# Chunk 1's q and k transposed by DMA instead of TensorE, with a new order of the work

## The chip, the cores and the metric

The kernel runs on one core of a Trainium2 chip. The metric is the device time of one execution in microseconds (us). A core has TensorE (matmuls and transposes; PE in the profile, PEld its weight loads), VectorE (DVE), ScalarE (ACT), GpSimd (POOL), SyncE (SP) and 16 DMA engines. SyncE, ScalarE and GpSimd each issue DMAs on a queue of their own (SPq, ACTq, POOLq).

## The reference, cut to what matters

A retention recurrence over 768 steps for 4 batches and 8 heads of 64, followed by a two-layer feed-forward with a tanh gelu over the 3072 tokens.

```python
for t in range(S):
    state = gamma[None, :, None, None] * state + np.einsum('bhd,bhe->bhde', k[:, :, t], v[:, :, t])
    y[:, :, t] = scale * np.einsum('bhd,bhde->bhe', q[:, :, t], state)
...
x = attn_out.transpose(0, 2, 1, 3).reshape(B * S, H * D)      # [3072, 512]
h = x @ w_in                                                   # [3072, 2048]
g = 0.5 * h * (1.0 + np.tanh(c * (h + 0.044715 * h * h * h)))
out = g @ w_out                                                # [3072, 512]
```

## The kernel before

**Tiling.** Time is cut into 6 chunks (c) of 128 steps; each chunk has 4 batches (b). w_in is cut into 4 column blocks and w_out into 4 row blocks (j). Inside a chunk, the recurrence is done as matrix work: a masked product of queries and keys, its product with the values, and the part that comes from the state. The 512 tokens of a chunk then go through the feed-forward. From chunk 0 (j = 2, 3) and chunk 1 on, both layers use a seven-product scheme for 2x2 blocks (sums of blocks ahead of the products); chunk 0 uses plain products for j = 0, 1 and for the second layer.

**The order.** The program is a string of words, ORDER (lines 16 to 138), read in the loop at lines 682 to 700. Each word calls one helper, which issues one or a few instructions. Nothing is reordered later: the place of a word in the string is the place of its instructions on their engine or queue, and an engine waits at an instruction until its inputs and its output buffer are there. A word's last letter V, A, P or S names DVE, ScalarE, GpSimd or SyncE; "@n" gives the buffer; "<word" adds a dependency on another word, used to keep GpSimd and DVE apart. The words of this study:

- L:q,c,b,e (line 330) loads 256 KB of q, k or v on queue e into one of 13 buffers "r". LC and LI load constants, LWI:j (262, two DMAs of 256 KB) and LWO:j (270, one of 512 KB) load a block of w_in or w_out on GpSimd's queue, where the fp32 weights become fp16. HOLD (296) is a two-element DMA.
- PREP (342) scales or converts a loaded tile to fp16; q and k of one (c,b) share a tile qk. EA multiplies by the decay mask (382, DVE).
- T:c,b (357) transposes q and k of one batch on TensorE, eight transposes of 128x128 into PSUM (a "bank"); ET (364) copies the result into the tile qkT. DT:c,b (367) does both with one DMA transpose on SyncE's queue, from qk to qkT. Before, chunks 0 and 1 use T and ET, chunks 2 to 5 use DT.
- A:c,b (374) is keys times queries from qkT, eight matmuls of half the rows. YP (390), YI (406) and SS (435) are the part from the state, the part inside the chunk and the state's update; EP, EY and ES copy their results.
- HB:j,b (486) is 16 matmuls of 128 columns, plain first layer for chunk 0. M1:c,j,n (539) is the n-th of seven products of the first layer, four matmuls of 256 columns; CP (567) and D1 (571) combine them, G and GB (575, 500) apply the gelu on ScalarE. O0:b,j (594) is the plain second layer of chunk 0, four matmuls of 512 columns; M2 (614) the second layer of the other chunks.
- WI, WO (320, 324) are sums of weight blocks, four per j and layer; SX and SG sums of blocks of x and g.
- ZERO and SPIN give TensorE 11 matmuls on zeros at the start.

All matmuls run through line 223, transposes on TensorE through 362, two-operand element work through 220, copies through 215 (ScalarE) and 217, gelu through 466, loads through 332, w_in through 266, w_out through 271, DMA transposes through 369.

**The order around the change.** First loads: SyncE takes k(0,1), constants, k(0,0), q(0,0), v(0,1), v(0,2); ScalarE q(0,1), k(0,2), q(0,2), q(0,3), k(0,3). GpSimd's queue takes, in order: LWI:2, v(0,0), v(0,3), LWI:0, LWI:3, LWI:1, then eight q and k of chunk 1, LWO:0, LWO:1, four v of chunk 1, LWO:2, k(2,3), q(2,3), LWO:3, seven loads of chunk 2. SyncE's own next words are three loads or holds and then DT of chunk 2.

Of the kernel before, what the change touches and what calls it, by code (L numbers as in the profile page):

```python
# [21 lines left out]
YI:0,1@5 EA:0,0,0 EA:0,2,0 PREP:v,0,0,A@2 A:0,3@2,7 L:k,1,0,P@12 EY:0,1,A@0 EA:0,3,0@3 YI:0,0@6 SS:0,0
YI:0,2@1 WI:2,1,P EY:0,0,A EA:0,3,1 SS:0,2@0 PREP:v,0,3,A@3 M1:0,2,1@4 EY:0,2,V M1:0,2,2@2 L:q,1,2,P@0
CP:0,2,11,V@0 SS:0,3 YI:0,3@5 WI:2,2,V L:k,1,1,P@5 HB:0,0@6 EY:0,3,A ES:0,1,A SX:0,1,V@0 L:q,1,3,P@4 HB:0,2@7
GB:0,0,0@0 SX:0,2,V@1 ES:0,0,V L:q,1,0,P@3 M1:0,2,5@1 GB:0,2,1@1 D1:0,2,11 HB:0,3@5 GB:0,2,0@2 L:k,1,2,P@1
SX:0,3,V@2 WI:3,1,V M1:0,2,6 WI:2,3,V M1:0,3,1@0 L:k,1,3,P@8 WI:3,3,V CP:0,2,12,A@1 M1:0,3,2@3 WI:3,2,V
GB:0,3,1 SX:0,4,V@3 HB:0,1@2 L:q,1,1,P@2 CP:0,3,11,A@2 WI:0,1,V G:0,2,11@3 WI:2,4,V M1:0,3,6 LWO:0 D1:0,3,11
M1:0,3,5@7 CP:0,3,12,A@3 PREP:k,1,0,V@4 M1:0,2,7 LWO:1 CP:0,2,22,A@0 HB:1,3@3 GB:0,1,0 L:v,1,1,P@6 D1:0,2,22
GB:0,3,0 M1:0,3,7 GB:0,1,1@4 PREP:k,1,1,V@0 G:0,3,11@5 L:v,1,0,P@7 M1:0,2,4 GB:1,3,1@6 PREP:q,1,2,V@1 HB:1,2@5
CP:0,3,22,A@2 L:v,1,2,P@11 PREP:q,1,3,V@2 GB:1,3,0@7 HB:1,0@2 GB:1,2,1 PREP:q,1,0,V L:v,1,3,P@9 HB:1,1@3  # L30
WI:3,4,V GB:1,0,0@8 GB:1,0,1@9 PREP:k,1,2,V G:0,2,21@10 M1:0,2,3 D1:0,3,22 GB:0,0,1 M1:0,3,3
# [5 lines left out]
PREP:v,1,3,P@4 YI:1,0 YI:1,1 SS:1,2@2 L:q,2,0,P@5 YI:1,2 EP:1,0,1,V@1 EP:1,0,0,A SS:1,0@7 SS:1,1 SS:1,3 YI:1,3
WO:0,2,V L:k,2,1,P@0 O0:2,0@5 ES:1,1,V EP:1,1,0,A EP:1,1,1,A L:k,2,2,P@4 M1:1,1,2@4 G:0,2,12@13 SX:1,1,V@4
M1:1,3,1@6 ES:1,0,V G:0,3,12@14 L:k,2,0,P@3 M1:1,1,1@0 CP:1,3,11,A@0 O0:2,1 SX:1,3,V@5 L:v,2,3,P@1
CP:1,1,11,A@1 M1:1,3,5@2 PREP:k,2,3,A@3 D1:1,1,11 M1:1,0,1@7 L:q,2,2,P@9 G:0,3,22@15 WI:1,1,V O0:1,2  # L40
CP:1,3,22,A@3 SX:1,2,V@1 L:v,2,0,P@6 SX:1,4,V@0 PREP:q,2,3,A M1:1,3,2@4 WI:1,3,V G:1,1,11@16 M1:1,3,6 WI:1,2,V
DT:2,3@1 O0:2,2 WI:0,2,V CP:1,3,12,A@1 WI:0,4,V CP:1,0,11,V@2 O0:0,2 WI:1,4,P<WI:0,4,V D1:1,3,11 M1:1,1,6
WO:3,1,V G:1,3,11@17 M1:1,3,3 WI:0,3,V O0:0,3 PREP:q,2,1,A@1 D1:1,3,12 PREP:k,2,1,P<WI:0,3,V M1:1,3,7
G:1,3,12@18 M1:1,0,6 CP:1,1,12,A@0 D1:1,3,22 M1:1,0,2@4 PREP:k,2,0,P@4 O0:2,3 G:1,3,22@19 D1:1,0,11
PREP:k,2,2,A@0 EO:0,V@0 M1:1,1,5@2 G:1,0,11@20 DT:2,1@2 M1:1,3,4 WO:3,2,V PREP:q,2,0,A M1:1,1,7 EO:2,V@1
M1:1,2,1@4 CP:1,0,12,A@1 PREP:v,2,0,P@0<WO:3,2,V CP:1,1,22,V@3 O0:1,3 PREP:q,2,2,A LD:S D1:1,1,22 DT:2,0@3
G:1,3,21@21 M1:1,0,5@1 WO:2,1,V EO:1,A@2 M1:1,1,4 WO:2,2,V CP:1,0,22,A@2 M1:1,1,3 SG:1,3,1,V@24 G:1,1,21@22
DT:2,2@4 M1:1,0,7 SG:1,3,3,P@25<SG:1,3,1,V D1:1,1,12 G:1,1,22@23 M1:1,2,5@5 D1:1,0,22 M1:1,0,3 L:q,3,3,A@7
PREP:v,2,2,P@2 G:1,1,12@26 A:2,3@6,3 L:v,2,1,S@11 D1:1,0,12 A:2,1@0,2 CP:1,2,11,A@3 L:k,3,3,S@12 M1:1,0,4
EA:2,3,0@2 SG:1,1,1,P@29 L:k,3,1,S@0 L:k,3,0,A@10 O0:3,0@1 EA:2,3,1 CP:1,2,22,A@0 G:1,0,21@27 O0:3,1  # L50
EA:2,1,0@0 SG:1,3,2,P@30 G:1,0,22@28 EA:2,1,1 A:2,0@6,7 L:q,3,0,S@3 A:2,2@3,0 WO:0,4,P EA:2,0,1@1 M1:1,2,6
# [25 lines left out]
SX:3,2,P@5<SX:3,1,V L:k,5,2,A@12 M1:3,1,2@3 PREP:q,4,3,A M1:2,2,3 ES:3,0,V SX:3,4,P@2 M2:1,4,1,0 CP:3,1,11,A@0
M1:2,2,7 D1:2,2,12 M1:3,0,1@2 PREP:v,4,1,P@0 D1:2,2,22 M1:3,0,2@6 G:2,2,12@34 M1:3,0,5@4 D1:3,1,11
PREP:v,4,3,P@3 CP:3,0,11,A@3 M1:3,1,6 L:v,4,0,A@11 M1:2,2,4 D1:3,0,11 PREP:k,4,1,A@3 SG:2,1,3,P@33 DT:4,2@1
M2:2,2,1,0 G:2,2,22@20 M1:2,2,2@3 M1:3,0,6 CP:3,0,22,A@1 SG:2,1,1,V@27 M2:1,4,1,1 SG:2,1,2,V@18 G:2,2,21@31  # L80
# [649 lines left out]
```

## Time and profile before

| | us |
|---|---|
| median of 3 runs | 194.16 (193.67 to 195.79) |
| the profiled execution | 195.35 |
| its span, first to last instruction | 192.2 |
| TensorE busy | 181.9 |
| DVE, GpSimd, ScalarE busy | 152.5, 123.9, 115.5 |
| DMA transposes | 16 |

In a row of the chain of waits or the timeline stand the start, the length, the engine, the line and the number of instructions. In a row of the groups, "out<-in" are tiles, "xN" the number, then busy time in us, mean in ns, and idle time ahead of them with what ended it. A row of the table of windows has the window, its length, the busy time of PE, PEld, DVE, ACT and POOL with their numbers of instructions, the granted clock, the DMA share and GB/s. "DMA to landing" is the time from a DMA's issue to its arrival, smallest, median and largest of the DMAs in the row above it.

### The profile page before, as it was taken

The numbers are of one execution on the slowest core, as the hardware profiler recorded it, in microseconds if no ns is written. First come the engines' busy times: TensorE is split into PE (matmuls) and PEld (weight loads), VectorE is DVE, ScalarE is ACT, GpSimd is POOL, SyncE is SP. The second block draws the span as 40 slices with busy tenths as digits, with TensorE's granted clock in tenths as the row PEclk, the third lists the DMA queues.
The fourth block names the chain that finished last, engine by engine and source line by source line (L and its number), as shares of the span: only waits on it lengthen the run. The fifth ranks groups of instructions, "written<-read, shape, count | busy, mean of one in ns | idle before, by whom it ended". The sixth has DMA issues, their size and how long they took to land.

```text
span 192.2 us, 5369 instructions
## 1 busy us (share of the span) xinstructions
PE 181.9 (95%) x2147; PEld 151.0 (79%) x2147; DVE 152.5 (79%) x305; ACT 115.5 (60%) x217; POOL 123.9 (64%) x132
## 2 busy tenths in 40 slices
...
PEclk9955999999999999999999999999999999999999
DMA  6999999999999999999999697480010030304053
GB/s 142 289 251 248 223 343 229 295 248 260 311 181 253 257 291 219 167 263 268 313 239 239 137 282 126 109 167 0 3 58 0 2 109 3 109 5 163 0 192 135
DMA packets 80540, 34.26 MB, mean 178 GB/s; under 512 B 69060, under 2 KB 78404, under 8 KB 80516
## 3 DMA queue, kind: packets, MB, share of 16 engines
...
q10 hardware_dynamic: 21856, 7.11, 14.7%
...
## 4 chain that ended last, share of the span: by engine, by line
PE 85%; DMA 5%; POOL 4%; ACT 2%; ACTq 1%; issue 1%; POOLq 0%
PE bank L223 84%; DMA r<-in_k_dram 3%; DMA qkT<-qk 2%; POOL w_in L266 2%; PE bank L362 1%; POOL qk L220 1%; POOL r L332 1%; ACT g L466 1%; ACT qk L215 1%; ACT qkT L215 1%; ACTq L332 0%; ACT o L215 0%; ACTq L231 0%; ACT h L215 0%; POOLq L220 0%
## 5 line engine op out<-in xcount | busy, mean ns | idle before, releaser
L223 PEld LDWEIGHTS <-g 128*128 128x128 f16 x624 | 60.4, 98 | 12.1 <-issue 0.2
L220 POOL TENSOR_TENSOR g<-g 128x512 f16<-128x512 f16 x45 | 51.3, 1156 | 26.8 <-DVE g L220 18.4
L223 PE MATMUL bank<-w_out,g 128*128 128x256 f16 (+1 forms) x384 | 58.3, 290 | 0.0
L220 DVE TENSOR_TENSOR h<-bank,h 128x512 f32<-128x512 f32 x66 | 43.8, 685 | 10.1 <-PE bank L223 5.3
L466 ACT ACTIVATE g<-h 128x512 f16<-128x512 f32 x66 | 40.2, 631 | 14.5 <-DVE h L220 10.7
L223 PEld LDWEIGHTS <-w_in 128*128 128x128 f16 x480 | 41.5, 98 | 5.3
L215 ACT COPY h<-bank 128x512 f32<-128x512 f32 x55 | 31.4, 586 | 15.3 <-PE bank L223 14.9
L223 PE MATMUL bank<-x,w_in 128*128 128x256 f16 (+1 forms) x304 | 32.4, 250 | 0.0
L223 PE MATMUL bank<-t_out,g 128*128 128x256 f16 x240 | 32.1, 273 | 0.0
L220 DVE TENSOR_TENSOR a<-bank,mask 128x512 f16<-128x512 f32 x48 | 29.9, 682 | 1.7 <-PE bank L223 1.6
L223 PEld LDWEIGHTS <-t_in 128*128 128x128 f16 x264 | 25.3, 98 | 4.1
L223 PE MATMUL bank<-sx,t_in 128*128 128x256 f16 x176 | 25.5, 273 | 0.0
L223 PE MATMUL bank<-sx,w_in 128*128 128x256 f16 x176 | 24.6, 273 | 0.0
L466 ACT ACTIVATE g<-bank 128x512 f16<-128x512 f32 (+1 forms) x38 | 18.4, 514 | 8.7 <-PE bank L223 8.5
L220 POOL TENSOR_TENSOR v<-r,cst 128x512 f16<-128x512 f32 x16 | 16.5, 1043 | 4.5 <-DMA r<-in_v_dram 2.6
L215 ACT COPY o<-bank 128x512 f32<-128x512 f32 (+1 forms) x18 | 9.3, 525 | 15.2 <-PE bank L223 15.2
L220 DVE TENSOR_TENSOR g<-g 128x512 f16<-128x512 f16 x35 | 15.3, 465 | 0.1
L220 DVE TENSOR_TENSOR o<-bank,o 128x512 f32<-128x512 f32 (+1 forms) x18 | 10.7, 598 | 4.6 <-PE bank L223 4.4
L215 ACT CAST qk<-r 128x512 f16<-128x512 f32 x20 | 12.3, 620 | 3.4 <-PE bank L223 1.6
L217 POOL CAST qk<-r 128x512 f16<-128x512 f32 x12 | 7.3, 610 | 9.8 <-PE bank L223 7.1
L223 PE MATMUL bank<-x,t_in 128*128 128x256 f16 x88 | 13.2, 273 | 0.0
L220 DVE TENSOR_TENSOR qk<-r,cst 128x512 f16<-128x512 f32 x13 | 8.6, 697 | 5.4 <-DMA cst<-rr_cst 4.3
(55 smaller groups left out, 181.9 us busy)
## 6 DMA issues: line engine op xcount, KB each, us to landing
...
```

The source lines that it names most:

```text
L215: did.append(nc.scalar.copy(out=out, in_=in_))
L217: did.append(EN[e].tensor_copy(out=out, in_=in_))
L220: did.append(EN[e].tensor_tensor(out=out, in0=in0, in1=in1, op=op))
L223: nc.tensor.matmul(out=out, lhsT=lhsT, rhs=rhs, start=start, stop=stop, skip_group_check=True)
L266: nc.gpsimd.dma_start(out=w_in[j][half * 64:(half + 1) * 64], in_=src[half, :, :, j * 512:(j + 1) * 512])
L332: EN[e].dma_start(out=t, in_=srcs[nm][b, :, c * C:(c + 1) * C, :].rearrange("h p d -> p h d"))
L362: nc.tensor.transpose(out=ps[:, i, hp], in_=t[:, i, hp], identity=iden)
L466: nc.scalar.activation(out=out, in_=in_, func=AF.Gelu_apprx_tanh, scale=1.0)
```

## The change

Only the string ORDER changes; the helpers are the same, four lines further up in the file (line 223 becomes 219).

- T:1,b and ET:1,b (b = 0 to 3) are gone; DT:1,b takes their place on SyncE's queue, ahead of SyncE's loads of chunk 2. The 32 transposes of chunk 1 and four copies (three on ScalarE, one on DVE) fall away; 20 DMA transposes stand where 16 were.
- The whole order is new. First loads: SyncE k(0,0), constants, v(0,1), k(0,1), q(0,0), v(0,2); ScalarE k(0,2), q(0,1), k(0,3), q(0,2), identity, q(0,3). GpSimd begins with PREP of k(0,0) and k(0,2), v(0,0), LWI:3, LWI:2, PREP:q,0,1, LWI:0, PREP:q,0,2, v(0,3), q(1,1), PREP:v,0,0, LWI:1, k(1,1), q(1,3), LWO:0, k(1,3), q(1,0), PREP:v,0,3, LWO:2, k(1,0), q(1,2), v(1,2), LWO:1, LWO:3, k(1,2), v(1,1), v(1,0).
- On TensorE, T:0,1 comes first (T:0,2 before), HB:0,0 is the first product of the first layer (M1:0,2,1 before), and chunk 1's first A stands behind all 8 HB, all 14 M1 of chunk 0 and seven O0, where it stood behind no O0.
- Work changes engines: WO nine times on GpSimd (four before), PREP of q(0,1) and q(0,2) on GpSimd, PREP of q(1,1) and k(1,3) too, and some loads of chunks 2 to 5 change queue. In all, words on DVE go from 140 to 129, on ScalarE from 141 to 142, on GpSimd from 116 to 125 (loads not counted).

The words of the start and around chunk 1's transposes, cut:

```diff
-L:q,0,1,A@0 L:k,0,1,S@1 ZERO LI:A LC:S SPIN:11@0 L:k,0,2,A@3 L:k,0,0,S@2 L:q,0,2,A@4 L:q,0,0,S@5 L:q,0,3,A@6
-L:v,0,1,S@8 L:k,0,3,A@7 PREP:q,0,1,V@0 L:v,0,2,S@11 MASK PREP:k,0,2,P@2<PREP:q,0,1,V TABLE LWI:2
-PREP:q,0,0,V@1 L:v,0,0,P@9 PREP:q,0,2,V L:v,0,3,P@10 PREP:k,0,1,V T:0,2@1 PREP:v,0,1,A@0 PREP:k,0,0,V T:0,1@2
...
-PREP:q,1,1,P<PREP:k,1,2,V GB:1,2,0 T:1,0@2 GB:1,1,0 D1:0,3,12 T:1,2@4 LWO:2 ET:1,0,A@4 L:q,2,1,S@2
-PREP:k,1,3,V M1:0,3,4 HOLD:0,0 T:1,1@7 L:k,2,3,P@10 ET:1,2,V@5 G:0,3,21@11 L:v,2,2,S@8 T:1,3@6 GB:1,1,1
...
+L:k,0,2,A@1 L:k,0,0,S@0 ZERO L:q,0,1,A@2 LC:S SPIN:11@0 L:k,0,3,A@7 L:v,0,1,S@3 L:k,0,1,S@4 L:q,0,2,A@8
+L:q,0,0,S@5 LI:A PREP:k,0,0,P@0 TABLE PREP:k,0,2,P@2 L:v,0,2,S@6 L:q,0,3,A@10 L:v,0,0,P@9 LWI:3 PREP:k,0,1,V@1
+LWI:2 PREP:q,0,1,P<PREP:k,0,1,V PREP:q,0,0,V LWI:0 T:0,1@1 MASK PREP:q,0,2,P<PREP:q,0,0,V ET:0,1,V@0
+L:v,0,3,P@11 A:0,1@2,3 L:q,1,1,P@12 T:0,2@4 EA:0,1,1@0 EA:0,1,0 PREP:v,0,0,P@2 T:0,0@5 LWI:1 WI:3,1,V
+PREP:q,0,3,V@3 PREP:v,0,2,A@0 PREP:k,0,3,V PREP:v,0,1,A@1 ET:0,2,A@1 ET:0,0,A@2 A:0,2@6,7 L:k,1,1,P@0 T:0,3@0
+EA:0,2,0@1 L:q,1,3,P@4 WI:2,1,V SS:0,1@1 ET:0,3,A@3 A:0,0@3,4 LWO:0 SS:0,2@2 EA:0,0,0@2 YI:0,1@5 L:k,1,3,P@1
+EA:0,0,1 A:0,3@6,3 EY:0,1,A@0 L:q,1,0,P@5 EA:0,2,1 YI:0,0@0 SS:0,0 EA:0,3,0@3 EY:0,0,A YI:0,2@4 PREP:v,0,3,P@3
+EA:0,3,1 HB:0,0@7 LWO:2 WI:2,2,V WI:3,2,V L:k,1,0,P@2 WI:3,4,V L:q,1,2,P@8 SS:0,3 GB:0,0,0@0 YI:0,3@5
+M1:0,3,1@0 EY:0,3,A L:v,1,2,P@6 HB:0,1@6 ES:0,1,A CP:0,3,11,V@0 ES:0,0,A LWO:1 WI:2,4,V M1:0,3,2@3 EY:0,2,A
+M1:0,2,1@5 LWO:3 GB:0,1,0 M1:0,2,2@2 SX:0,1,V@0 GB:0,1,1@1 HB:0,3@1 CP:0,2,11,A@1 L:k,1,2,P@3 D1:0,2,11
...
+G:0,3,11@7 M1:0,2,5@4 PREP:k,1,1,V@2 L:v,1,0,P@7 M1:0,2,6 GB:0,3,0 GB:0,2,1 SX:0,3,V@3 O0:1,0@7 GB:1,1,1
+CP:0,3,22,V@2 CP:0,2,12,A@1 CP:0,2,22,V@3 GB:1,1,0 M1:0,3,3 O0:2,0@1 PREP:k,1,0,V WI:3,3,V DT:1,0@4 M1:0,2,3
+CP:0,3,12,V@0 PREP:v,1,2,P@4<WI:3,3,V M1:0,2,7 O0:0,0@2 PREP:q,1,1,P D1:0,2,22 D1:0,3,12 M1:0,3,7 PREP:k,1,3,P
+M1:0,2,4 D1:0,3,22 HB:1,3@6 L:v,1,3,P@9 WI:0,1,V G:0,3,22@8 WI:0,2,V O0:1,1 G:0,3,12@9 WO:0,1,V DT:1,1@5
+D1:0,2,12 M1:0,3,4 WI:1,2,V HB:1,2@3 G:0,2,12@10 PREP:k,1,2,V@0 GB:1,3,1@11 GB:1,3,0@12 O0:1,2 WI:0,4,V
+G:0,2,21@13 WI:0,3,V G:0,2,22@14 O0:1,3 PREP:q,1,2,V GB:1,2,0 G:0,3,21@15 WO:2,1,V O0:0,1 DT:1,3@6 WO:1,1,V
+EO:1,A@0 PREP:v,1,1,P@5<WO:1,1,V GB:1,2,1 A:1,0@4,6 PREP:v,1,0,P@6 O0:0,2 EA:1,0,1@0 DT:1,2@0 WI:1,3,P
+EA:1,0,0 A:1,1@5,6 YP:1,0@0,4 L:k,2,2,P@5 EA:1,1,1@2 L:q,2,1,S@11 SS:1,0@7 SS:1,1 L:k,2,0,S@6 YI:1,0 EA:1,1,0
+L:q,2,2,P@4 L:k,2,1,S@2 A:1,3@3,6 YI:1,1 EA:1,3,0@1 O0:2,1 WO:3,1,P EP:1,0,1,A@1 EP:1,0,0,V L:q,2,0,S@3
...
```

More of the change, by code (lines that the diff above doesn't have):

```diff
@@ L22 @@
[L22 to L31, printed above, removed]
@@ L37 @@
[L37 to L46, printed above, removed]
@@ L47 @@
[L47 to L51, printed above, removed]
@@ L77 @@
[L77 to L80, printed above, removed]
-M2:1,4,0,1 L:v,5,0,S@4 D1:2,2,11 PREP:q,4,1,P<SG:2,1,2,V G:3,0,11@26 M2:2,1,0,0@6 DT:4,3@4 SX:3,3,V@4
@@ new lines @@
+D1:1,0,11 M1:1,3,2@2 PREP:q,2,2,A@4 ES:1,1,V M1:1,1,6 G:1,0,11@16 M1:1,3,6 PREP:k,2,1,P<SX:1,3,V G:1,1,11@17
+D1:1,3,11 O0:2,3 PREP:k,2,2,P CP:1,1,12,A@2 DT:2,1@1 CP:1,3,12,V@0 O0:3,0@6 SX:1,4,P@1 EO:2,A@2 L:k,3,3,A@9
+M1:1,0,5@3 G:1,3,11@18 WO:1,2,V L:v,2,1,S@7 M1:1,3,7 PREP:q,2,3,P@2<WO:1,2,V PREP:q,2,0,A@1 DT:2,2@2
+M1:1,1,5@2 D1:1,3,22 M1:1,1,7 WO:0,2,P CP:1,1,22,V@1 M1:1,3,3 G:1,3,22@19 M1:1,3,4 D1:1,1,22 PREP:k,2,3,P
+CP:1,0,22,A@3 M1:1,1,3 D1:1,3,12 PREP:k,2,0,P M1:1,0,6 G:1,1,22@20 M1:1,1,4 D1:1,1,12 PREP:v,2,0,P@1
@@ new lines @@
+EA:2,2,0 A:2,0@5,4 M1:1,2,3 SG:1,0,1,P@30 EA:2,0,0@1 M1:1,2,2@3 EA:2,0,1 M1:1,2,7 L:q,4,2,S@12 EO:3,A@3
+PREP:v,2,2,P@3 YP:2,0@7,2 D1:1,2,11 YP:2,1@5,4 YI:2,0 D1:1,2,22 YI:2,1 G:1,2,11@31 SG:1,0,3,P@34 SS:2,0@3
+YI:2,2 EP:2,0,0,V@0 G:1,0,12@32 SS:2,2@6 L:v,3,3,S@2 SS:2,1 YI:2,3 PREP:q,3,2,A@0 SS:2,3 EP:2,0,1,V
+SG:1,3,3,P@38 M2:1,2,0,0@7 G:1,2,22@33 D1:1,2,12 M1:1,2,4 L:v,3,2,A@10 M2:1,1,0,0@2 EP:2,1,1,V PREP:q,3,1,P@1
+HOLD:1,2 G:1,2,21@36 M2:1,1,1,0 SG:1,1,2,V@35 L:q,3,0,A@7 M1:2,0,1@0 EP:2,1,0,V G:1,2,12@37
@@ new lines @@
+L:q,4,3,S@5 D1:2,0,22 WO:0,4,P<SX:2,4,V PREP:k,3,3,A M1:2,0,3 CP:2,3,22,V@2 M1:2,3,7 G:2,0,22@10 DT:3,3@6
+M1:2,0,4 D1:2,0,12 WO:0,3,P PREP:k,3,0,A@3 M2:1,6,1,0 D2:1,11, CP:2,1,11,A@3 M1:2,3,3 SG:1,2,4,P@2
+PREP:q,3,0,A D1:2,3,22 M1:2,1,5@6 M1:2,1,2@1 D1:2,3,12 G:2,3,22@7 M2:1,6,0,1 PREP:v,3,2,P@6 D1:2,1,11
+G:2,0,21@9 DT:3,0@1 M1:2,3,4 M1:2,1,6 G:2,3,21@6 SG:1,2,3,V@11 A:3,1@7,0 SG:2,0,3,V@13 CP:2,1,22,A@2 A:3,2@3,1
+L:k,4,1,S@6 SG:1,1,4,V@8 M2:1,5,0,0@4 G:2,0,12@14 EA:3,1,0@1 ST0:1,S PREP:v,3,3,P@5<SG:1,1,4,V M2:1,5,1,0
@@ new lines @@
+G:2,1,11@15 L:k,4,2,S@9 EA:3,2,1@0 M1:2,1,3 L:q,4,0,S@3 CP:2,1,12,A@0 M2:1,5,0,1 SG:1,0,4,P@12 EA:3,1,1
+M2:1,5,1,1 EA:3,2,0 L:v,4,0,S@7 M1:2,1,7 CO:1,22,A@5 WO:2,3,P D1:2,1,12 M2:1,6,1,1 PREP:q,4,1,A@2 A:3,3@7,1
+D1:2,1,22 A:3,0@0,3 L:k,4,3,A@0 PREP:v,3,1,P@7 M2:1,3,0,0 EA:3,3,1@2 L:v,4,1,S@10 G:2,1,22@27 M2:1,3,1,0
+EA:3,0,1@3 G:2,1,12@22 PREP:v,3,0,P@4 M2:1,3,1,1 M2:1,3,0,1 CO:1,12,A@1 EA:3,0,0 L:v,4,2,S@11 M1:2,1,4
+WO:1,3,P D2:1,12, YP:3,0@6,1 G:2,1,21@18 YP:3,1@3,0 EA:3,3,0 YI:3,2 G:2,3,12@17 WO:3,3,P YI:3,0 L:q,5,1,S@4
@@ new lines @@
+YI:3,1 L:v,4,3,A@2 SS:3,3@5 SS:3,1@4 EP:3,0,1,V@1 SS:3,0 L:k,5,2,A@1 YI:3,3 SG:2,1,3,P@21 SS:3,2
+PREP:q,4,3,A@4 EP:3,1,1,V M1:2,2,5@7 HOLD:1,3 PREP:k,4,2,A@1 M1:2,2,1@1 L:k,5,1,S@5 EP:3,1,0,V M1:2,2,2@0
+WO:2,4,P CP:2,2,11,A@3 EP:3,0,0,V M2:1,7,0,0 PREP:k,4,1,A L:k,4,0,S@9 M2:1,7,1,0 ES:3,1,V SX:3,1,P@1 ST:1,12,A
+M2:2,1,0,0@3 CP:2,2,22,A@2 M1:2,2,6 ES:3,0,V M1:3,1,1@6 SX:3,2,P@0 CP:2,2,12,A@0 M2:1,7,0,1 L:q,5,0,S@6
+PREP:k,4,3,A M2:1,7,1,1 SG:2,1,1,V@24 PREP:q,4,2,A M1:2,2,7 D1:2,2,11 SG:2,1,2,P@26<SG:2,1,1,V M1:2,2,3
```

163 lines of the change are left out of this document (77 added, 86 removed).

## The prediction

> **What bounds the kernel now.** I read the page first (span, busy shares, slices), then the chain of waits, then the table of windows, then the timeline of the start and the DMA rows.
>
> ```profile
> span 192.2 us, 5369 instructions
> PE 181.9 (95%) x2147; PEld 151.0 (79%) x2147; DVE 152.5 (79%) x305; ACT 115.5 (60%) x217; POOL 123.9 (64%) x132
> PEclk9955999999999999999999999999999999999999
> DMA  6999999999999999999999697480010030304053
> ```
> ```profile
> 16.98 15.54 PE bank L223 x234
> 32.52 0.89 PE bank L362 x16
> ...
> 33.85 0.89 PE bank L362 x16
> 34.74 18.27 PE bank L223 x220
> ...
> 57.01 4.78 DMA qkT<-qk
> ...
> 61.83 91.32 PE bank L223 x1168
> ...
> 153.16 35.55 PE bank L223 x324
> ...
> 188.73 0.37 ACT o L215
> ```
> ```profile
> 12.55:17.00 4.45, 3.41 (x51) 2.43 (x52) 4.28 (x7) 1.08 (x2) 4.45 (x8) 0.50 1.18 257
> 62.00:80.00 18.00, 18.00 (x240) 15.19 (x235) 17.20 (x40) 12.89 (x24) 11.73 (x12) 1.00 1.18 241
> 36.00:46.00 10.00, 10.00 (x157) 6.41 (x155) 9.42 (x23) 7.98 (x15) 8.02 (x10) 1.00 1.16 251
> ```
>
> From about 19 us to 188.73 us TensorE is the bound: the chain lies on it almost throughout and its windows are full. Every wait that TensorE does not have today lengthens the kernel one for one; every matmul removed shortens it one for one. Ahead of 19 us lies a start that DVE and GpSimd set (granted clock 0.50 until 17 us). DMA stands at nine tenths or more from slice 2 to about 100 us, so a transfer added early has no free engine time. The 57 us DMA step of the chain cost TensorE little: it is a transpose of chunk 2 that came just in time.
>
> **Part 1, the gain.** The two rows of L362 with 16 instructions are all 32 transposes of chunk 1, 0.89 + 0.89 = 1.8 us, on the bound. The four copies qkT out of PSUM (three ACT, one DVE) also go; neither engine was the bound, so I count nothing. If nothing else changed, the time would fall by 1.8 us. The tail after the last matmul keeps its shape (ScalarE copy, store), so nothing there.
>
> **Part 2, the start.**
>
> ```profile
> 5.41 0.69 DVE L220 TENSOR_TENSOR qk<-r,cst 128x512 f16<-128x512 f32 x1 [4.28 <-DMA cst<-rr_cst]
> 7.43 1.04 POOL L220 TENSOR_TENSOR qk<-r,cst 128x512 f16<-128x512 f32 x1 [6.98 <-DMA r<-in_k_dram]
> 8.41 1.44 POOL L266 DMA_DIRECT2D w_in<-in_moe_w_in_dram  x2
> 9.82 1.83 POOL L332 DMA_DIRECT2D r<-in_v_dram  x2
> 9.88 2.74 PE L362 MATMUL bank<-iden,qk 128*128 128x128 f16 x24 [4.12 <-DVE qk L220]
> 10.95 1.01 ACT L215 COPY qkT<-bank 128x1024 f16<-128x1024 f16 x1 [0.30 <-PE bank L362]
> 13.27 3.67 DVE L220 TENSOR_TENSOR a<-bank,mask 128x512 f16<-128x512 f32 x6
> 18.95 1.05 PE L223 MATMUL bank<-x,w_in 128*128 128x256 f16 x8
> ```
>
> Before, TensorE's first transposes start at 9.88 and its first M1 at 18.95. After, T:0,1 is first and needs PREP:q,0,1, which GpSimd now makes behind PREP:k,0,0, PREP:k,0,2, one load and two LWI: 5.4 + 1.05 + 1.05 + 0.9 + 1.4 + 1.4 + 1.05 = 12.3 us, 2.4 us later. PREP:q,0,2 follows LWI:0 and ends at 14.7, so T:0,2 and T:0,0 (0.9 each at half clock) run to 16.5; DVE must then do EA twice, WI, two PREP, T:0,3 gets its keys at 18.0, ScalarE's copy 1.0 later, and with four more EA (0.6 to 0.7 each) YI:0,0 can run at about 20.5, HB:0,0 at 21.6. I take 21.6; from 18.95, that is 2.65 us later for the same remaining work.
>
> **Part 3, what TensorE meets next.** Prices on TensorE:
>
> ```profile
> 20.40 1.96 PE L223 MATMUL bank<-x,w_in 128*128 128x128 f16 x32
> 22.19 0.60 PE L223 MATMUL bank<-sx,t_in 128*128 128x256 f16 x4
> ...
> 42.41 1.47 PE L223 MATMUL bank<-x,w_in 128*128 128x256 f16 x12
> 43.72 1.03 PE L223 MATMUL bank<-w_out,g 128*128 128x512 f16 x4
> 44.59 0.60 PE L223 MATMUL bank<-sx,t_in 128*128 128x256 f16 x4
> ```
>
> By the starts: two HB take 22.19 - 20.40 = 1.79 (0.9 each), three M1 43.72 - 42.41 = 1.31 (0.44 each), one O0 0.87. Between HB:0,0 and A:1,0 the new order has 8 HB, 14 M1, 7 O0 and 0.4 us of small work: 7.1 + 6.1 + 6.0 + 0.4 = 19.7, so A:1,0 would come at 41.3 without a wait. But the new order brings weights and loads differently on GpSimd's DMA queue, and that queue lands its transfers one by one:
>
> ```profile
> L271 POOL DMA_DIRECT2D w_out<-in_moe_w_out_dram x2: 777/778/780, 26.1 to 26.9; - x2
> DMA to landing us min/median/max: 7.9/8.8/9.7
> L332 POOL DMA_DIRECT2D r<-in_v_dram x4: 889/922/947, 27.6 to 31.2; - x4
> DMA to landing us min/median/max: 8.6/9.2/9.7
> ```
>
> Before, w_out 0 lands at 26.1 + 7.9 = 34.0 and w_out 1 at 26.9 + 9.7 = 36.6: 2.5 us for one. The four v land from 27.6 + 9.7 = 37.3 to 31.2 + 8.6 = 39.8: 0.8 us each. At 36.6 that queue had moved all of w_in, two w_out and ten loads. After, k(1,0) stands behind w_in, two w_out and seven loads, so it lands two loads earlier, at 35.0; w_out 1 stands behind one w_out more, at 39.1; w_out 3 at 41.6; k(1,2) at 42.4.
>
> ```profile
> L220 DVE TENSOR_TENSOR h<-bank,h 128x512 f32<-128x512 f32 x66 | 43.8, 685 | 10.1 <-PE bank L223 5.3
> L466 ACT ACTIVATE g<-h 128x512 f16<-128x512 f32 x66 | 40.2, 631 | 14.5 <-DVE h L220 10.7
> ```
> ```profile
> L220 DVE TENSOR_TENSOR t_in<-w_in,t_in 128x512 f16<-128x512 f16 x7 | 2.9, 420 | 0.0
> ```
>
> With 0.7 us for a D1, CP or PREP on DVE, 0.4 for a weight sum and 0.6 for a G: DVE stops at PREP:k,1,0 until 35.0. Behind it are WI:3,3 and CP:0,3,12, for which M1:0,3,7 waits: 35.0 + 0.7 + 0.4 + 0.7 = 36.8; then D1:0,2,22 (37.5), M1:0,2,4, HB:1,3 (38.9), and O0:1,1 waits for w_out 1 until 39.1. DVE goes on with two D1, three weight sums and D1:0,2,12, 3 x 0.7 + 3 x 0.4 = 3.3, to 40.8; ScalarE's G 0.6 more; O0:1,2 starts at 41.5 and, after it, O0:1,3 and O0:0,1 bring A:1,0 to 44.1. The late start of part 2 disappears in these waits, it is not added to them.
>
> **Part 4, the four DMA transposes.** They are queued on SyncE while GpSimd's queue is still full.
>
> ```profile
> L369 SPq DMA_TRANSPOSE qkT<-qk x12: 1240/1796/3532, 71.8 to 124.2; - x12
> DMA to landing us min/median/max: 2.8/4.5/8.1
> ```
> ```profile
> L332 SPq DMA_DIRECT2D r<-in_q_dram x1: 367/367/367, 33.2 to 33.2; - x1
> DMA to landing us min/median/max: 13.4/13.4/13.4
> ```
>
> Later in the kernel a transpose lands 2.8 to 8.1 us after its issue, median 4.5, and SyncE spends 1.8 us on its issue. But the one load that SyncE issued at 33.2, into the same traffic, took 13.4 us, where GpSimd's loads of the same size landed 0.8 us apart. DT:1,0 (issued about 36) should land by 40.5 at the median and by 49 at the bad row; DT:1,2 needs PREP:k,1,2 (42.4 + 0.7), two weight sums and PREP:q,1,2, and is issued at 44.7, when GpSimd's queue is nearly drained (its last v at 44.8). I therefore take the median there, 49.2; ends 47.5 and 52.8. A:1,0 to A:1,2 is 3.5 us of TensorE work, so without DT:1,2 A:1,2 would stand at 47.7: the transpose is 1.5 us late. The q and k loads of chunk 2 that SyncE now holds are queued behind these four transposes, too; TensorE reaches chunk 2's A some 13 us later, which covers a 4.5 us landing after them.
>
> The Trainium skill, page "DMA: Bandwidth & Descriptors", section "Queues, rings and completion order", says that each DMA engine serves its queues in turn, a packet at a time; the 13.4 us beside 0.8 us agrees, and it speaks against moving work here. The same page, section "Latency and other measured facts", gives 261 GB/s for a DMA transpose; an estimate from that is 1.0 us for 256 KB, with which the transposes would be no wait and the sum would end at part 3.
>
> **Sum.** M1:1,1,1 starts at 49.2 + 0.3 = 49.5. Before, the first M1 of chunk 1 stood at 42.41 and 188.7 - 42.4 = 146.3 us of TensorE followed. In the new order four more O0 are done by then (4 x 0.87 = 3.5) and 1.0 us of YP, YI and SS not yet (half of the 2.09 us in the next row): 143.8.
>
> ```profile
> 39.45:41.54 2.09, 2.09 (x97) 1.91 (x97) 1.72 (x4) 0.96 (x2) 1.69 (x3) 1.00 1.20 235
> ```
>
> TensorE ends at 49.5 + 143.8 = 193.3, which is 4.6 later. The profiled execution took 195.35 (its span 192.2 and 3.15 around it) and would become 199.95. The runs' median is 194.16, 1.2 below it, so I forecast 194.16 + 4.6 = 198.8. Of later stages I count no change: the moved weight sums (nine WO on GpSimd, four before) and other new pairings lie beside a TensorE that has been full.
>
> **The rivals.**
> - *Transposes hidden, weights and DVE late only* (A:1,2 at 47.7): 48.0 + 143.8 = 191.8, +3.1, 197.3. The 2.8 us row speaks for it, the 13.4 us row against it.
> - *Transposes starved* like the 13.4 us load (DT:1,2 at 52.8): +8.2, 202.4. GpSimd's chunk 2 loads could restart the traffic; against it, that queue should be drained near 45.
> - *Only the late start counts*, loads land in time: 2.65 - 1.8 = +0.85, and part of that is filled: 194.2 to 195.0, no change. It needs w_out 1 by 37.
> - *Faster*: GpSimd's queue runs ahead, so that k(1,0) is there by 33 and w_out 1 by 35, the start is no later than before, and the transposes hide behind O0 as they do for chunks 3 to 5, where the trace shows no wait of TensorE on them: -1.8, 192.4. It decides if w_out 1 lands 4 us earlier than the row spacing gives; for it, seven O0 stand ahead of A:1,0, where none stood before; against it, 251 GB/s and a DMA share above 1 in the window 36 to 46.
>
> **How the numbers follow.** Chances: forecast 0.42, transposes hidden 0.20, starved 0.12, only the start 0.13, faster 0.13. The range 193.5 to 202.5 leaves out the faster case and half of the starved one, 0.19. The forecast's own range, with its two neighbours, is 196.2 to 202.5. One per cent, about what a measurement of this kernel tells from no change, is 192.2 and 196.1: faster 0.13, within 0.13, slower 0.74.
>
> **What would show it.** First L362 matmul at about 12.3 and first M1 past 22; TensorE idle before an O0 near 39 with w_out as releaser, DVE idle on k's load near 35; TensorE idle before chunk 1's A on DMA qkT between 44 and 50; last matmul near 193. If TensorE is full from 20 us to the end with no DMA releaser, parts 3 and 4 are wrong; if a wait appears after 70 us, my claim that later stages keep their fill is wrong.

## The result and the profile after

| | before | after |
|---|---|---|
| median of 4 runs, us | 194.97 (193.67 to 196.68) | 205.84 (205.38 to 206.60) |
| the profiled execution | 195.35 | 205.53 |
| its span | 192.2 | 203.8 |
| last matmul ends | 188.71 | 200.51 |

After takes 1.0571 times as long as before (95% interval 1.0521 to 1.0621), 10.9 us more. The forecast was 198.8, with 202.5 as the upper end of the range: the sign was right, the time fell outside. A correction to the list of the change: the helpers do not stand four lines further up; the profile after has the line numbers of before. And two details of that list: GpSimd made PREP of q(1,1) before, too, and the words counted for ScalarE and GpSimd include their loads.

The page of after, the same rows as were shown of before:

```profile
span 203.8 us, 5297 instructions
PE 183.6 (90%) x2115; PEld 149.8 (74%) x2115; DVE 154.7 (76%) x294; ACT 111.4 (55%) x211; POOL 132.8 (65%) x141
PEclk9855899998599999999999999999999999999999
DMA  6999999999995999999999999042400011203244
```

The 32 transposes are gone (2147 matmuls became 2115), yet TensorE is busy 1.7 us longer in all, and fills 90% of the span instead of 95%. The granted clock has a second dip, in slices 9 and 10, counted from 0 (46 to 56 us). The chain of waits of after, from chunk 1 on:

```profile
36.98 1.07 POOL qk L220 x2
38.05 13.09 DMA qkT<-qk
...
51.18 149.32 PE bank L223 x1751
```

The chain of before ran on TensorE almost throughout from 17 us; here it leaves TensorE and passes through one DMA transpose of 13.09 us. From 51.18 us to the end the chain stays on TensorE, so no later wait adds to the loss; the lower clock of the next 5 us, shown below, does. The DMA rows of chunk 1's transposes, the first one alone, then the three behind it:

```profile
L369 SPq DMA_TRANSPOSE qkT<-qk x1: 1344/1344/1344, 35.6 to 35.6; - x1
DMA to landing us min/median/max: 12.2/12.2/12.2
```
```profile
L369 SPq DMA_TRANSPOSE qkT<-qk x3: 1382/2342/7172, 38.0 to 47.8; - x3
DMA to landing us min/median/max: 13.1/13.1/13.1
```

The first two, DT:1,0 and DT:1,1, land 12.2 and 13.1 us after their issue (47.8 and 51.1). The issue of DT:1,3 alone holds SyncE for 7.2 us, so DT:1,2 is issued only at 47.8. TensorE's timeline at that place:

```profile
41.44 2.86 PE L223 MATMUL bank<-w_out,g 128*128 128x512 f16 x12
47.84 0.40 PE L223 MATMUL bank<-qkT 64*128 64x128 f16 x8 [3.55 <-DMA qkT<-qk]
...
51.18 0.61 PE L223 MATMUL bank<-qkT 64*128 64x128 f16 x8 [1.97 <-DMA qkT<-qk]
...
56.54 0.61 PE L223 MATMUL bank<-x,w_in 128*128 128x256 f16 x4
```

A:1,0 waits 3.55 us, A:1,1 another 1.97. M1:1,1,1, the mark of the prediction's sum, starts at 56.54 where 49.5 was forecast. The windows across it:

```profile
42.00:46.00 4.00, 2.30 (x11) 0.77 (x8) 2.63 (x6) 2.44 (x6) 0.17 (x1) 1.00 1.53 115
...
47.00:49.30 2.30, 1.37 (x12) 0.54 (x12) 1.01 (x2) 0.00 (x0) 2.30 (x3) 1.00 1.16 224
49.30:56.10 6.80, 4.92 (x68) 2.75 (x68) 3.45 (x6) 1.12 (x2) 5.40 (x6) 0.50 1.28 230
```

The window 42 to 46 is the one to read: the DMA engines are fuller than in the other windows shown (share 1.53) and move only 115 GB/s, less than half of the 251 GB/s that before had between 36 and 46. And from 49.3 to 56.1 us the granted clock is 0.50.

### The profile page after: what moved, and what is told of

It reads as the page before. It is cut to its first block, busy times and chain, and to the rows that moved or that the text cites. A ratio compares the mean times of both kernels' runs of the same rounds, so it can differ in the third digit from the quotient of the medians.

```text
span 203.8 us, 5297 instructions
## 1 busy us (share of the span) xinstructions
PE 183.6 (90%) x2115; PEld 149.8 (74%) x2115; DVE 154.7 (76%) x294; ACT 111.4 (55%) x211; POOL 132.8 (65%) x141
## 4 chain that ended last, share of the span: by engine, by line
PE 73%; DMA 17%; POOL 6%; issue 1%; SPq 0%; ACT 0%; POOLq 0%
PE bank L223 73%; DMA qkT<-qk 6%; DMA r<-in_k_dram 4%; DMA r<-in_v_dram 4%; POOL qk L220 3%; DMA cst<-rr_cst 2%; POOL w_in L266 2%; POOL r L332 1%; POOL v L217 0%; SPq L332 0%; ACT o L215 0%; POOLq L332 0%; POOLq L217 0%; POOLq L220 0%
## 5 line engine op out<-in xcount | busy, mean ns | idle before, releaser
L220 POOL TENSOR_TENSOR g<-g 128x512 f16<-128x512 f16 x46 | 52.6, 1162 | 27.6 <-DVE g L220 11.2
L220 DVE TENSOR_TENSOR a<-bank,mask 128x512 f16<-128x512 f32 x48 | 30.7, 683 | 9.2 <-PE bank L223 9.1
L215 ACT COPY h<-bank 128x512 f32<-128x512 f32 x50 | 29.1, 588 | 14.3 <-PE bank L223 13.3
L223 PE MATMUL bank<-t_out,g 128*128 128x256 f16 x240 | 32.8, 273 | 0.0
L223 PE MATMUL bank<-sx,w_in 128*128 128x256 f16 x176 | 25.3, 273 | 0.6 <-DVE h L217 0.6
L215 ACT COPY o<-bank 128x512 f32<-128x512 f32 (+1 forms) x21 | 11.2, 535 | 16.8 <-PE bank L223 16.8
L220 DVE TENSOR_TENSOR g<-g 128x512 f16<-128x512 f16 x34 | 17.7, 544 | 0.1
L223 PE MATMUL bank<-qkT 64*128 64x128 f16 x192 | 10.0, 239 | 8.0 <-DMA qkT<-qk 5.5
L220 POOL TENSOR_TENSOR v<-r,cst 128x512 f16<-128x512 f32 x16 | 16.5, 1044 | 1.0 <-DVE g L220 1.0
L223 PEld LDWEIGHTS <-qkT 64*128 64x128 f16 x192 | 6.1, 102 | 13.3 <-DMA qkT<-qk 6.5
L220 DVE TENSOR_TENSOR qk<-r,cst 128x512 f16<-128x512 f32 x10 | 6.6, 687 | 11.9 <-DMA r<-in_k_dram 9.4
```

The lines of the kernel that those rows point to most:

```text
L215: did.append(nc.scalar.copy(out=out, in_=in_))
L220: did.append(EN[e].tensor_tensor(out=out, in0=in0, in1=in1, op=op))
L223: nc.tensor.matmul(out=out, lhsT=lhsT, rhs=rhs, start=start, stop=stop, skip_group_check=True)
```

## The experiments

Twelve kernels were run. Each time stands beside the median of before on the same chip. In the expectations, theory A of the first runs is that transposes by DMA land late because GpSimd's loads share the DMA engines with them; its rival is that the price is the transposes' own.

**TensorE's transposes put back in the new order** (against after):

```diff
-DT:1,0@4
+T:1,0@6 ET:1,0,A@4
-DT:1,1@5
-HB:1,2@3
+HB:1,2@3 T:1,1@4 ET:1,1,A@5
-DT:1,3@6
+T:1,3@5 ET:1,3,A@6
-DT:1,2@0
+T:1,2@3 ET:1,2,A@0
```

> The new order with the transposes of chunk 1 back on TensorE. Theory A (the DMA transposes land late because GpSimd's loads share the DMA engines with them): without them TensorE waits only for w_out 1 near 39 and for k(1,2) near 43; A:1,0 at 44 to 46, M1:1,1,1 near 49.5 instead of 56.5, no drop of the clock, about 199 us. Rival B (the new order itself costs, whoever transposes): 204 us or more.

204.63, before 195.24 (1.0479, 1.0412 to 1.0546). That is the rival's time, but not yet for its reason: the clock stayed at 1.0 from 24 us, and the way the copies were put in made waits of its own. ET:1,1 stood on ScalarE ahead of a G that O0:1,2 needs (TensorE waits 1.4 us), and T:1,2 took a bank still in use (0.6 us). It says nothing yet on the order; the second attempt is below.

**DMA transposes put into before's order** (against before):

```diff
-T:1,0@2 T:1,2@4 T:1,1@7 T:1,3@6
-ET:1,0,A@4 ET:1,2,V@5 ET:1,1,A@6 ET:1,3,A@0
+DT:1,0@4 DT:1,2@5 DT:1,1@6 DT:1,3@0
```

> The order of before with the four transposes of chunk 1 by DMA at the places of the copies, and nothing else changed. Theory A: issued from about 33 on into GpSimd's full queue, the first lands 10 us or more after its issue and TensorE, which has only O0 behind them in the order, waits 10 to 15 us before chunk 1's A: 205 to 210 us. Rival C (a DMA transpose is late only in the new order): landing 4.5 us, about 199 us.

212.31, before 195.24 (1.0894, 1.0803 to 1.0985). What TensorE waits for in it, the DMA transpose that ends the long wait (DT:1,2), and two of its windows:

```profile
PE bank L223 <- DMA qkT<-qk: 15.8, 2, 15.5
```
```profile
L369 SPq DMA_TRANSPOSE qkT<-qk x1: 5068/5068/5068, 39.9 to 39.9; - x1
DMA to landing us min/median/max: 8.2/8.2/8.2
```
```profile
32.00:48.00 16.00, 0.64 (x6) 0.32 (x4) 2.13 (x3) 3.69 (x8) 3.70 (x5) 0.61 1.20 228
48.00:52.50 4.50, 4.37 (x24) 1.82 (x24) 2.82 (x5) 0.00 (x0) 2.61 (x4) 0.50 0.78 142
```

Without the seven O0 in front, TensorE stands for 16 us. So the replacement by itself, in before's order and traffic, costs 17 us, more than the theory's 205 to 210. Not all of the wait is a late landing. The first transpose, DT:1,0, was issued at 30.3 and, by the updates of its semaphore in the trace, landed near 44.3, 14.0 us later, as the theory has it. But TensorE waits for DT:1,2, which lands 8.2 us after its issue, and that issue came only at 39.9: ahead of it SyncE stood 6.0 us at the issue of a HOLD (0.7 us in before).

**Less traffic on GpSimd's queue** (against after; w_out 1 and 3 are not loaded but set to zero at the start, so half of the second layer's weights is left out):

```diff
-LWO:1
-LWO:3
+for j in (1, 3):
+    nc.vector.memset(w_out[j], 0.0)
```

> The changed kernel without the loads of w_out 1 and 3 (1 MB each of 34 MB; zeros are written there instead by DVE at the start, so half of the second layer is left out of the result's value). Theory A: GpSimd's queue is drained 5 to 6 us earlier, the first transpose lands 5 to 8 us after its issue instead of 12.2, A:1,0 near 43, A:1,2 near 47, about 197 us. Rival C (four transposes in a row take their 12 us by themselves): landing still 12 us after issue, 204 us.

198.01, before 195.24 (1.0148, 1.0079 to 1.0217). DT:1,0 in it, and TensorE's timeline at the place (the file has two lines more, so L371 is L369):

```profile
L371 SPq DMA_TRANSPOSE qkT<-qk x1: 1351/1351/1351, 35.7 to 35.7; - x1
DMA to landing us min/median/max: 4.1/4.1/4.1
```
```profile
44.24 0.40 PE L223 MATMUL bank<-qkT 64*128 64x128 f16 x8
...
45.54 0.40 PE L223 MATMUL bank<-qkT 64*128 64x128 f16 x8
...
48.64 0.40 PE L223 MATMUL bank<-qkT 64*128 64x128 f16 x8
48.97 0.61 PE L223 MATMUL bank<-x,w_in 128*128 128x256 f16 x4
```

The transpose is issued at the same time as in after (35.74, 35.62) and lands in 4.1 us instead of 12.2. All of GpSimd's loads of chunk 1 but v(1,3) are in by 38.7 in this run, by 44.8 in after. No matmul waits for a transpose, the clock has no second dip, and M1:1,1,1 starts at 48.97, 7.6 us earlier. That is shown: the transposes' late landing is the traffic's doing. A price of 12 us of their own is ruled out; at most some 4 are their own.

**The clock kept up by matmuls on zeros** (against after):

```diff
-A:1,0@4,6
+SPIN:16@4 A:1,0@4,6
-A:1,1@5,6
+SPIN:9@5 A:1,1@5,6
```

> The changed kernel with 16 matmuls on zeros ahead of A:1,0 and 9 ahead of A:1,1, where TensorE waits, and nothing else. Theory A with the clock as a second cost: the granted clock stays at 1.00 between 49 and 56, the transposes land as before, and 2 to 2.5 us of the 5 us at half clock come back: about 203.5 us. Rival: the third and fourth transposes are then the limit and nothing comes back, 205.5 us.

205.89, before 195.24 (1.0544, 1.0471 to 1.0618): the same as after. TensorE's timeline in it (L258 is SPIN), and the window that was at half clock in after:

```profile
49.02 2.11 PE L258 MATMUL bank<-zero 128*128 128x512 f16 x9
51.78 0.40 PE L223 MATMUL bank<-qkT 64*128 64x128 f16 x8 [0.66 <-DMA qkT<-qk]
...
55.70 0.40 PE L223 MATMUL bank<-qkT 64*128 64x128 f16 x8 [0.76 <-DMA qkT<-qk]
56.03 0.61 PE L223 MATMUL bank<-x,w_in 128*128 128x256 f16 x4
```
```profile
49.30:56.10 6.80, 5.34 (x86) 2.76 (x85) 3.41 (x6) 0.59 (x1) 6.17 (x7) 1.00 1.22 219
```

The clock stays at 1.00, and M1:1,1,1 comes only 0.5 us earlier: at full clock A:1,2 meets its own transpose, which has not landed before 55.7. The half clock is a consequence that costs time only where nothing else is late. The rival was right.

**TensorE's transposes in the new order, better placed** (against after):

```diff
-DT:1,0@4
+T:1,0@6 ET:1,0,A@4
-HB:1,2@3
+HB:1,2@3 T:1,1@4 ET:1,1,V@5
-DT:1,3@6
+T:1,3@5 ET:1,3,V@6 T:1,2@0 ET:1,2,A@0
-DT:1,1@5
-DT:1,2@0
```

> The new order with the transposes on TensorE again, this time placed so that no copy out of PSUM stands ahead of the gelu that O0:1,2 needs (in the first trial that copy cost 1.6 us, and a PSUM bank still in use another 0.8). Theory A (waits for the DMA transposes and the clock that drops in them cost about 8 us, the late start about 5): M1:1,1,1 at 51 and 201 us or less, still some 5 us above the kernel before, all of it from the start. Rival B (something else in the new order costs): M1:1,1,1 at 51 and the time still 204 us, lost again behind it.

201.89, before 195.46 (1.0331, 1.0279 to 1.0383). Its window over chunk 1's A, and its M1:1,1,1:

```profile
42.00:56.00 14.00, 13.95 (x211) 9.23 (x208) 12.27 (x26) 8.23 (x18) 8.80 (x10) 1.00 0.77 198
```
```profile
51.28 0.61 PE L223 MATMUL bank<-x,w_in 128*128 128x256 f16 x4
```

TensorE is full there, M1:1,1,1 is 5.3 us earlier than in after. This splits the loss: the new order with TensorE's transposes is 6.4 us slower than before; the DMA transposes add the rest of the 10.9, some 4.4 us net. Since they also save 1.8 us of TensorE, their late landing, with the clock behind it, costs some 6.2 us by these medians (7.6 by M1:1,1,1 of the run with less traffic).

**Four of GpSimd's loads moved to ScalarE's queue** (against after):

```diff
-L:k,1,2,P@3 L:v,1,1,P@10 L:v,1,0,P@7 L:v,1,3,P@9
+L:k,1,2,A@3 L:v,1,1,A@10 L:v,1,0,A@7 L:v,1,3,A@9
```

> The changed kernel with the last four loads of chunk 1, k(1,2) and three v, on ScalarE's queue instead of GpSimd's; bytes and transposes unchanged. Theory A1 (a transpose is slow while GpSimd's queue holds anything): that queue ends with w_out 3 near 39, the first transpose lands by 43 and the fourth by 48, M1:1,1,1 near 50 to 52, 200 us. Rival A2 (any bytes of that amount slow it): landing still near 47, 205 us.

203.56, before 195.46 (1.0402, 1.0349 to 1.0456). Its DT:1,0:

```profile
L369 SPq DMA_TRANSPOSE qkT<-qk x1: 1356/1356/1356, 36.0 to 36.0; - x1
DMA to landing us min/median/max: 9.3/9.3/9.3
```

9.3 us, between 4.1 and 12.2; the time lies between the two theories' 200 and 205. The weights were still on GpSimd's queue, so this does not tell whether the kind of queue matters or only the amount. Open.

**The start: q(0,1) prepared on DVE first** (against after):

```diff
-PREP:k,0,1,V@1
+PREP:q,0,1,V@1 PREP:k,0,1,V
-PREP:q,0,1,P<PREP:k,0,1,V
```

> The changed kernel with PREP:q,0,1 on DVE ahead of PREP:k,0,1 instead of on GpSimd behind four w_in transfers; the first TensorE transpose should start near 9 to 10 instead of 12.4. Theory A (the late start is hidden by the wait for the DMA transposes, whose time the GpSimd queue sets): the start moves by 1 us or more, and the time by 0.5 us at most, 205.5 us. Rival (the start counts in full): 203 to 204 us.

205.70, before 195.46 (1.0513, 1.0457 to 1.0569). The issue of the identity matrix and TensorE's first transposes in it:

```profile
5.54 2.67 ACTq L231 DMA_DIRECT2D iden<-rr_ident  x1
12.10 1.01 PE L362 MATMUL bank<-iden,qk 128*128 128x128 f16 x8 [6.32 <-DMA iden<-rr_ident]
```

A miss that taught something: the first transpose stays at 12.1, held now by the identity matrix, which the new order put fifth on ScalarE's queue. The identity has to move too.

**That done, with TensorE's and with DMA's transposes** (against the better placed one and against after):

```diff
-L:q,0,1,A@2
+L:q,0,1,A@2 LI:A
-PREP:k,0,1,V@1
+PREP:q,0,1,V@1 MASK PREP:k,0,1,V PREP:q,0,2,V
...
-LI:A
-PREP:q,0,1,P<PREP:k,0,1,V
-MASK
-PREP:q,0,2,P<PREP:q,0,0,V
```

> The new order with the transposes on TensorE (as in the placed trial) and the start mended: the identity second on ScalarE's queue as before (it landed at 12.1 and held the first transpose in the trial with PREP:q,0,1 on DVE), the mask and PREP of q(0,1) and q(0,2) on DVE ahead of GpSimd's transfers. Theory A (what is left of the loss is the start): first transpose near 9.5, HB:0,0 near 20 instead of 22.3, the time 3 to 5 us lower than the placed trial's 201.9: 197 to 199 us. Rival (GpSimd's queue, which lands k(1,0) near 35.5 in either case, holds DVE and TensorE there): HB:0,0 earlier, but M1:1,1,1 still near 51, 201 us.

> The changed kernel, with its DMA transposes, and the same mended start. Theory A (the transposes wait for k(1,0), that lands near 35, and then for their own slow landing near 47 and 51, whatever TensorE did earlier): the start moves by 2 us or more, A:1,0 stays at 47 to 48 and M1:1,1,1 at 56, 205.5 us; the idle time goes from the start to chunk 1's A. Rival (start and transposes add up): 202 to 203.5 us.

With TensorE's transposes 202.16, before 194.29 (1.0389, 1.0329 to 1.0450); with DMA's 205.87, before 194.29 (1.0540, 1.0418 to 1.0662). TensorE in the first of them:

```profile
7.98 0.38 PE L362 MATMUL bank<-iden,qk 128*128 128x128 f16 x4 [1.91 <-DMA iden<-rr_ident]
...
21.57 1.77 PE L223 MATMUL bank<-x,w_in 128*128 128x128 f16 x16
...
23.79 0.32 PE L223 MATMUL bank<-v,qk 128*64 128x64 f16 x8 [0.46 <-POOL v L217]
```

The first transpose is 4.3 us earlier than in the better placed kernel (12.29), HB:0,0 only 0.7 (22.25), and SS:0,3, which waits for v(0,3) from GpSimd's queue in both, 0.8 (24.56). M1:1,1,1 stands at 51.53, no earlier than 51.28 without this: what was left of the gain went into a longer wait (1.6 us, 0.5 without this) of a later M1 for DVE's copies of chunk 0. With DMA transposes A:1,1 waits until 50.96 (51.18 in after), for a transpose that lands at 50.91. So in after the late start is hidden behind the transposes.

**GpSimd's queue in another order, with TensorE's and with DMA's transposes** (against the better placed one and against after): v(0,3) and w_in 0 earlier, k(1,0) ahead of the second w_out, w_out 1 before w_out 2. The words of that queue, without the words of other engines between them (PREP:v,0,3 and WI:2,1 move with their loads):

```diff
-L:v,0,0,P@9 LWI:3 LWI:2
+L:v,0,0,P@9 L:v,0,3,P@11 LWI:3 LWI:0
...
+LWI:2 PREP:q,0,2,P<PREP:q,0,0,V
...
-LWO:2 L:k,1,0,P@2 L:q,1,2,P@8 L:v,1,2,P@6 LWO:1 LWO:3 L:k,1,2,P@3
+L:k,1,0,P@2 LWO:1 L:q,1,2,P@8 L:k,1,2,P@3 L:v,1,2,P@6 LWO:2 LWO:3
```

> The new order with the transposes on TensorE (as in the placed trial) and GpSimd's queue put in the order in which the work needs it: v(0,3) and w_in 0 earlier, k(1,0) ahead of the second w_out, w_out 1 ahead of w_out 2, k(1,2) earlier. Theory A (what the new order loses beside the transposes is the landing order of that queue): v(0,3) no longer holds SS:0,3, k(1,0) lands near 32.5, M1:1,1,1 near 49 to 49.5 instead of 51.3, 199.5 to 200.5 us. Rival (the queue is not it): 202 us.

> The same queue order with the DMA transposes. k(1,0) is there some 2 us earlier and the first transpose can be issued near 33.5. Theory A (landing is slow as long as GpSimd's queue holds anything, until about 45): the first transposes still land at 45 to 47 and M1:1,1,1 comes near 55 to 56, 204 to 205.5 us, so 4 to 5 us above its twin with the transposes on TensorE. Rival (an earlier issue carries over one for one): 2 to 3 us less than the changed kernel, 203 us.

With TensorE's transposes 202.74, before 195.97 (1.0284, 1.0154 to 1.0414): no gain over 201.89. Two rows of its timeline:

```profile
33.10 1.90 DVE L220 TENSOR_TENSOR qk<-r,cst 128x512 f16<-128x512 f32 x3 [3.70 <-DMA r<-in_q_dram]
...
35.99 1.01 PE L223 MATMUL bank<-sx,w_in 128*128 128x256 f16 x4 [3.46 <-DVE h L217]
```

The queue's start is quicker, but the same bytes stand in it: DVE now waits 3.7 us for q(1,0), and the CP behind that wait holds TensorE for 3.5 us, after which the granted clock is 0.50 from 35.5 to 38.9. With DMA's transposes 203.03, before 195.97 (1.0364, 1.0267 to 1.0460), 2.8 us less than after (3.8 by the differences to before). That is the rival's time, but not by an earlier issue: k(1,0) lands 2.6 us earlier (32.18), DVE gets to it late, and DT:1,0 is issued at 35.50, 0.1 us earlier than in after. It takes 10.3 us instead of 12.2.

**A longer SPIN in before**, to see whether the clock at the start matters (before, `SPIN:11@0` becomes `SPIN:30@0`):

> The kernel before with 30 instead of 11 matmuls on zeros at the start, so that TensorE is busy until its first transposes at 9.9. If the half clock between 8.7 and 19 us lengthens the start: the clock stays at 1.00 and 0.5 to 1.5 us are gained, 193.5 to 194.5 us. If the start is set by DVE, ScalarE and GpSimd alone: no change, 195 us.

194.99, before 195.46 (0.9989, 0.9957 to 1.0021): no difference. The clock holds until 14.6 us and is 0.5 from there to 21.5; TensorE waits for DVE and GpSimd around that place (1.9 us at the longest), and its first M1 starts where it did.

No version was faster than before.

## Why the prediction was wrong

**What bounds it, and part 1, right.** TensorE is the bound outside the start and chunk 1; 32 matmuls less came out as counted. From M1:1,1,1 to the last matmul 143.8 us were forecast, 144.0 measured (56.54 to 200.51): no new wait in any later stage. One error was hidden by chance: the last matmul came 7.2 us after its forecast of 193.3, the profiled execution only 5.6 us after its 199.95, because the 3.15 us around the span that the sum carried over were 1.7 in after.

**Part 2, the start: the right place, the size too small.** The first transpose was forecast at 12.3 and started at 12.37; HB:0,0 was forecast at 21.6 and came at 23.19. The wait for the first transpose and the start's timeline of after:

```profile
PE bank L362 <- POOL qk L220: 6.8, 1, 6.8
```
```profile
10.83 1.48 POOL L220 TENSOR_TENSOR qk<-r,cst 128x512 f16<-128x512 f32 x1
11.33 3.64 DVE L247 TENSOR_SCALAR mask<-cst 128x128 f32<-128x128 f32 x8
13.54 1.07 POOL L220 TENSOR_TENSOR qk<-r,cst 128x512 f16<-128x512 f32 x1
...
15.63 0.61 PE L223 MATMUL bank<-qkT 64*128 64x128 f16 x8 [2.23 <-DVE qkT L217]
16.17 1.89 PE L362 MATMUL bank<-iden,qk 128*128 128x128 f16 x16
...
23.19 1.00 PE L223 MATMUL bank<-x,w_in 128*128 128x128 f16 x15
```

The term left out is MASK on DVE. Its eight instructions took 1.17 us in before, at 6 to 7 us, when GpSimd did nothing; here they lie beside GpSimd's PREPs and DMA issues and take 3.64. ET:0,1 stands behind them on DVE, A:0,1 waits 2.23 us for ET:0,1, and T:0,2 and T:0,0, behind A:0,1, end at 18.1 where 16.5 was forecast, as much as the 1.6 us by which HB:0,0 was missed. No run moved MASK alone. The better placed kernel starts with the same words and has HB:0,0 at 22.25, so this place differs by 0.9 us between runs.

**Part 3, the landings of weights and keys: right.** Forecast and measured: k(1,0) 35.0 and 34.8, w_out 1 39.1 and 38.7, w_out 3 41.6 and 42.4, k(1,2) 42.4 and 43.1, the end of O0:0,1 44.1 and 44.3. That O0:1,1 would wait for w_out 1 was not so: TensorE came there late by itself, at 39.25. DVE's wait for k(1,2) is in the timeline of after:

```profile
43.13 0.69 DVE L220 TENSOR_TENSOR qk<-r,cst 128x512 f16<-128x512 f32 x1 [2.10 <-DMA r<-in_k_dram]
```

**Part 4 failed: the landing of the transposes.** For DT:1,0 it named two ends, 40.5 by the median of 4.5 us of later transposes and 49 by the 13.4 us of a SyncE load that ran in this traffic; its sum then went by DT:1,2 alone, at the median, because GpSimd's queue should be nearly drained by then. Measured were 12.2 and 13.1 us for DT:1,0 and DT:1,1: the near row, in time and in traffic, was the 13.4. The next load that SyncE issued in before, not shown in the prediction, took longer still:

```profile
L332 SPq DMA_DIRECT2D r<-in_v_dram x1: 381/381/381, 34.5 to 34.5; - x1
DMA to landing us min/median/max: 19.5/19.5/19.5
```

The later transposes, of which 4.5 us was the median, run at 72 to 124 us, when GpSimd issues no DMA in before's timeline. Nor was GpSimd's queue drained: its last v, forecast at 44.8, was issued at 38.97 and landed at 51.1. DT:1,2, on which the sum hung, was issued at 47.8 instead of 44.7, behind the 7.2 us issue of DT:1,3, and was not the one waited for: A:1,2 starts at 56.21 without a wait.

With the run without w_out 1 and 3 as a base, in which nothing waits for a transpose, the sum closes: M1:1,1,1 there at 48.97, plus 3.55 for A:1,0, plus 1.97 for A:1,1, plus 1.93 for the half clock (the stretch from A:1,1 to M1:1,1,1 takes 5.36 us in after, 3.43 there) gives 56.42; measured 56.54. Of these 7.45 us part 4 had 1.5. The base itself stands 1.0 us later than the 48.0 forecast without a wait for transposes. Most of that is part 4's, too: it put A:1,0 to A:1,2 at 3.5 us, and they take 4.4 there (44.24 to 48.64). Parts 2 and 3 had A:1,0 at 44.1, and TensorE was free for it at 44.3 in after.

The second thing missing in part 4 is the clock. After a wait of 3.55 us and most of a second one, the granted clock goes to 0.50 at 49.3. The Trainium skill, page "TensorE: Matmul & The Clock Gate", part 1, says that an idle window of about 3.4 us puts TensorE back to half rate. The 16 us in before's order agree, and here the fall comes behind a wait of 3.55 us. But in the kernel with DMA's transposes and GpSimd's queue in another order the clock fell at 50.4, and the waits just before were 0.73 and 1.18 us, TensorE being busy for 1.53 of the 3.4 us from 47.0 on; so no idle stretch of 3.4 us was needed there:

```profile
47.92 0.40 PE L223 MATMUL bank<-qkT 64*128 64x128 f16 x8 [0.73 <-DMA qkT<-qk]
...
50.44 0.61 PE L223 MATMUL bank<-qkT 64*128 64x128 f16 x8 [1.18 <-DMA qkT<-qk]
```

No run here was made to find the bound. The run with matmuls on zeros showed that this term could not have been saved by itself.

The page "DMA: Bandwidth & Descriptors" of the Trainium skill, section "Queues, rings and completion order", has each DMA engine serve its queues in turn. The 12.2 us with and 4.1 us without GpSimd's traffic agree. The 261 GB/s that its section "Latency and other measured facts" gives for a DMA transpose with a non-contiguous middle dimension, 1.0 us for 256 KB as an estimate, is not what a kernel sees even with that traffic nearly gone: 4.1 us from issue to landing.

**The rivals.** "Transposes starved" had the mechanism, and 202.4 for it; it had it for DT:1,2 only and without the clock. Its price was that of the 8.1 us row (44.7 + 8.1 = 52.8) and not of the 13.4 us in its name, by which DT:1,2 would have stood at 58.1. "Hidden" and "faster" were wrong, and "only the late start counts" too: moving the start changed nothing with either kind of transpose.

**What stays open.** The new order costs 6.4 us with TensorE's transposes. In that kernel's trace 3.3 of it stand at HB:0,0 (18.95 in before, 22.25 there; 23.19 in after) and 1.25 at SS:0,3, the rest in waits of under 1 us each. But the attempts to take it away, at the start and in GpSimd's queue, each brought the next wait. That GpSimd's queue as a whole is the reason is argued from these, not shown.
